# A pre-norm attention and gated MLP block: the down projection of two token tiles from seven block products, the start in another order, and all steps ordered by a table

## The chip, the cores and the metric

The kernel runs on one core of a Trainium2 chip. The metric is the device time in microseconds (us) of one execution. The time before is the median of 3 runs, 788.14 us (785.44 to 790.55). Engines are named as in the profile: PE is TensorE (PEld its weight loads), DVE is VectorE, ACT is ScalarE, POOL is GpSimd, SP issues the DMAs.

## What is computed

The reference, cut to what matters (T = 2048 tokens, D = 512, 32 heads of 16, F = 1376, float32 throughout):

```python
def _A_ref(x, wqkv, wo):              # H = 32; Dh = 16; W = 256
    qkv = (x @ wqkv).reshape(B, S, 3, H, Dh).transpose(2, 0, 3, 1, 4)
    q, k, v = qkv[0], qkv[1], qkv[2]
    scores = jnp.einsum("bhqd,bhkd->bhqk", q, k) * (Dh ** -0.5)
    mask = (idx[:, None] - idx[None, :] >= 0) & (idx[:, None] - idx[None, :] < W)
    p = _softmax(jnp.where(mask[None, None], scores, -1e9), axis=-1)
    o = jnp.einsum("bhqk,bhkd->bhqd", p, v)
    return o.transpose(0, 2, 1, 3).reshape(B, S, D) @ wo

def _B_ref(x, w_gate, w_up, w_down):
    return (_sigmoid(x @ w_gate) * (x @ w_up)) @ w_down

h = x + _A_ref(_layernorm(x), A_wqkv, A_wo)
h2 = h + _B_ref(_layernorm(h), B_w_gate, B_w_up, B_w_down)
```

## The kernel before, in words

**Numbers.** Each float32 matrix product is made of three float16 matmuls: both sides are scaled by a power of two, rounded to a high half, and the remainder is the low half; the products high·high, high·low and low·high are summed in PSUM (`mm3`). So each operand needs a rounding (a cast) and a subtraction, and each weight an absolute maximum first (`bound`, `scale`).

**Stages.** Tokens are in 16 tiles of 128. The start loads x and the weights of q, k, v and o, takes the maxima, normalises and transposes the first tiles on PE. `do_ln`, `do_qk`, `do_v` go over blocks of 256 tokens; `do_s` (scores for the row maxima), `do_st` (scores again, exponentials), `do_pv`, `do_o` and `do_wo` make attention, and `do_wo` leaves x + attention in X, which holds all 16 tiles on the chip. From the middle of this stage on, the weights of gate, up and down are read (`do_amax`), and gate and up are split into halves. The last pool (`open_p2`) opens when attention's buffers are free: the rest is gate, up and down, for pairs of token tiles.

**Gate and up.** `do_ln2` normalises the two tiles of a pair; `do_pair(p, c)` goes over three parts c of F (512, 512 and 352 columns) and gets gate and up of both tiles, a 2 x 2 block product, from seven products of combined blocks instead of eight (the Strassen and Winograd way): seven products of six matmuls each, whose PSUM banks are copied or added into tiles of SQ by ACT and DVE (`copied`, `added`). `gated` applies the sigmoid on ACT, multiplies on DVE or POOL, splits the result into halves in a tile `hr`, and transposes it by DMA into a place `hT`: one transpose for a token tile and part, 48 in all.

**Down.** `do_down(t)` goes over the 11 blocks of F (ten of 128 rows and one of 96) for one token tile: three matmuls of 512 columns each in one PSUM bank (ring `mm`, two banks), then one DVE instruction (L1099) that adds X and writes to RH, and the DMA out. `do_split(n)` loads one such block of w_down and splits it into halves (ACT and DVE, `halves`).

**The order.** The kernel is written as generators; each `yield` states the engines that could do the next step with a cost, what it needs, and the rings of buffers that it takes. `Planner.run` goes through them and takes, at each time of its own clock, the step with the lowest priority number that can start; priorities come from constants `C` and a table of shifts `SHIFT`. The engines' queues are then fixed in that order and run in order, with semaphores between them. Where several engines could do a step, `alt` allows it for the names in `C["alts"]`. Rings: 3 chunks for weights on their way, 3 tiles `hr`, 3 places for normalised pairs (X2).

**The start.** POOL sets constants in the order in which the text has them: the mask, ones in VT, zeros in `mh`, the identity, then zeros for the staging tiles `sq` and for SQ (`zeros`, `clear`, L411 and L417). `normal` computes mean and variance on DVE, and the power −1/2 on POOL (L478); `prep` takes the maxima of a weight (L293 on ACT, L295 on DVE) and splits it (L452, L454).

Of the kernel before, what the change touches and what calls it, by code (L numbers as in the profile page):

```python
# [26 lines left out]
F32 = mybir.dt.float32  # L27
# [24 lines left out]
AHEAD = 2  # L52

PE_, DVE_, ACT_, POOL_, DMA_ = ENGINES = "PE", "DVE", "ACT", "POOL", "DMA"

C = dict(zero=-46.373, s=7.211, pv=-31.68, o=-67.24, wo=[13.21, 53.452], v=[23.818, 127.681], qk=[-13.459, 6.441], ln=[-31.38, -5.584], m=-39.786, am=243.064, amd=116.487, sp=[132.972, 8.062], l2=[-53.459, -314.47], ngu=4, gu=[255.313, 151.063], sp2=[-37.338, 31.729], l2b=-29.57, eps=0.065, prep=[-249.121, -79.126, -27.448, -187.12], alts=['amax', 'cp', 'hhi', 'hi', 'less2', 'lo', 'oadd', 'pt', 'qk', 'raw', 'v', 'whi', 'wsc'], look=-0.248, blog=291.066, bias={'ACT': -74.105, 'DVE': -28.406, 'POOL': -183.807}, pet=8, npv=2, down=167.802, lw=[-144.266, -82.209, -44.544, 78.782], lx=[134.236, 99.816], fill=[197.218, 182.462], clear=69.714, write=-203.887, slack=132.421, stack=-165.218, off={'ln': [-160.407, -74.442, -3.855, -33.644, 18.117, 88.024, 134.307, 85.825], 'qk': [-37.42, -19.282, 102.973, 30.571, 156.591, 137.001, 38.026, 42.788], 'v': [159.08, 126.771, 137.631, -91.406, 127.637, 151.976, 86.279, 51.768], 's': [-65.666, 11.728, -23.007, 22.514, -27.425, -30.856, 15.823, -16.406], 'wo': [59.674, -28.634, 34.768, 157.532, 71.738, 193.098, 45.03, -20.162], 'o': [-100.642, 202.197, -157.044, -26.171, 77.762, -0.239, 84.539, 28.44], 'pv': [-118.465, -136.9, 28.841, -162.287, 81.069, -58.225, 116.111, -106.813], 'm': [120.536, -271.105, -196.395, -173.5, -275.023, 110.942, -102.738, -139.801]}, ld=-120.453, sq=[-52.631, -19.855], slg=-2.394, la=[26.407, 18.616])


SHIFT = [
# [28 lines left out]
]  # L88

LAG = {"PE": 0.2, "DVE": 0.2, "ACT": 0.19, "POOL": 0.1, "DMA": 0.0}  # L90
OWN = {"PE": 0.0, "DVE": 0.06, "ACT": 0.05, "POOL": 0.0, "DMA": 0.0}
TICK = 10.24 / 3
SWITCH = 0.095


class Port(float):
    pass


class Planner:  # L100

# [1148 lines left out]
```

## Time and profile before

| what | us |
|---|---|
| median of 3 runs | 788.14 (785.44 to 790.55) |
| the profiled execution's own time | 787.88 |
| its span in the trace | 786.1 |
| PE, DVE, ACT, POOL busy | 743.5, 557.9, 460.7, 320.6 |
| first matmul of the transposes, first q/k matmul | 11.93, 18.02 |
| first row maximum | 53.35 |
| last pool opens | 467.17 |
| last matmuls begin, last evacuation begins | 780.24, 782.38 |

The profile shows one execution on the chip. Busy times are unions of the intervals of an engine's instructions; "x" is a count; a row of slices shows tenths of the busy share in 40 equal parts of the span. A row of the timeline has the start, the length, the engine, the line, the operation with its tiles, and in brackets the idle time before it and what ended it; instructions of one kind that follow each other stand in one row with their count. A row of the groups has busy time and mean length in ns, then the engine's idle time just before them and the releasers.

### The profile page before, as it was taken

How to read it: one execution, taken by the hardware profiler on the slowest of the kernel's cores; microseconds unless marked ns; L12 is line 12 of the kernel's file. 1: busy time of each engine (PE TensorE's matmuls, PEld its weight loads, DVE VectorE, ACT ScalarE, POOL GpSimd, SP SyncE). 2: the span in 40 equal slices, each digit the busy share in tenths (PEclk: the TensorE clock that was granted, in tenths of full speed). 3: DMA queues.
4: the chain of work that ended last, by engine and by line, in shares of the span. 5: the costliest groups of instructions: out<-in, count | busy, mean ns of one | idle time of the engine just before them, and what ended most of it. 6: DMA issues, size and time to landing. Idle time of an engine off the chain costs nothing.

```text
span 786.1 us, 17989 instructions
## 1 busy us (share of the span) xinstructions
PE 743.5 (95%) x6606; PEld 460.9 (59%) x6606; DVE 557.9 (71%) x1682; ACT 460.7 (59%) x801; POOL 320.6 (41%) x390
## 2 busy tenths in 40 slices
PE   2899989999999999999999997899999999999998
PEld 1577758678777676777655553454454544544453
DVE  5879999959999899999799448885346434613431
ACT  5851768768878878798877647572335223502330
POOL 9731345444645645565569643504304400400000
PEclk9999999999999999999999999999999999999999
DMA  9387393483946999858985429885426521521321
GB/s 327 115 245 213 99 165 68 123 188 93 200 105 180 189 232 234 177 141 189 255 203 103 70 41 281 163 189 96 100 54 92 111 60 28 95 67 40 61 58 42
DMA packets 179383, 107.99 MB, mean 137 GB/s; under 512 B 144288, under 2 KB 153504, under 8 KB 179296
## 3 DMA queue, kind: packets, MB, share of 16 engines
q1 hardware_dynamic: 179296, 106.86, 58.8%
q8 instruction: 51, 0.84, 0.5%
q14 instruction: 36, 0.29, 0.1%
HBM read 42.07 MB, written 17.83 MB: 76 GB/s over the span
## 4 chain that ended last, share of the span: by engine, by line
PE 64%; DVE 12%; issue 8%; ACT 7%; DMA 5%; POOL 3%; DVEq 0%; POOLq 0%; ACTq 0%; SPq 0%
PE mmp L328 24%; PE sp L998 13%; PE pvp L745 7%; PE sp L654 6%; PE stp L998 5%; DVE junk L639 3%; PE pvp L998 2%; PE stp L719 2%; PE stp L709 2%; DMA oT<-whl 2%; DMA x<-hl 2%; PE stp L708 1%; ACT pa L684 1%; DVE mq L639 1%; PE stp L710 1%
## 5 line engine op out<-in xcount | busy, mean ns | idle before, releaser
L639 DVE CUSTOM_DVE_ANT_0 junk<-sp,mask 128x320 bf16<-128x320 f32 (+4 forms) x512 | 207.4, 464 | 13.7 <-PE sp L654 13.3
L684 ACT ACTIVATE pa<-stp,kappa 128x512 f32<-128x512 f32 (+1 forms) x256 | 155.0, 645 | 22.0 <-PE stp L710 18.8
L998 PEld LDWEIGHTS <-x 128*128 128x128 f16 x1008 | 98.2, 98 | 105.1 <-issue 5.4
L998 PE MATMUL sp<-W,x 128*128 128x512 f16 (+1 forms) x612 | 133.2, 361 | 2.1 <-DVE SQ L1021 2.1
L654 PE MATMUL sp<-SK,SQ 96*128 96x256 f16 (+2 forms) x960 | 127.2, 232 | 5.8 <-DVE mq L639 2.7
L328 PE MATMUL mmp<-xT,W 128*128 128x256 f16 x768 | 111.6, 277 | 5.6 <-DVE W L454 2.2
L654 PEld LDWEIGHTS <-SQ 96*128 96x128 f16 x960 | 80.9, 97 | 34.8 <-issue 16.1
L684 ACT ACTIVATE pb<-stp,kappa 128x512 f32<-128x512 f32 x128 | 83.0, 685 | 13.5 <-PE stp L719 12.2
L692 POOL TENSOR_SCALAR_AFFINE_SELECT pa<-pa 128x1024 f32<-128x1024 f32 x56 | 61.4, 1096 | 70.9 <-ACT pa L684 70.7
L328 PEld LDWEIGHTS <-W 128*128 128x128 f16 x768 | 70.8, 99 | 18.3 <-DVE W L454 3.4
L478 POOL TENSOR_TENSOR rs<-rs,nhalf 128x1 f32<-128x1 f32 x32 | 21.7, 685 | 145.5 <-DVE rs L475 142.8
L281 ACT ACTIVATE SQ<-sp 128x512 f32<-128x512 f32 (+1 forms) x45 | 24.4, 544 | 80.1 <-PE sp L998 79.7
L745 PE MATMUL pvp<-pa,VT 128*17 128x128 f32 (+1 forms) x1408 | 62.7, 308 | 0.0
L998 PE MATMUL stp<-W,x 128*128 128x512 f16 (+1 forms) x264 | 57.4, 355 | 3.8 <-DMA W<-wr 2.6
L709 PE MATMUL stp<-SQ,SK 100*128 100x256 f16 x224 | 59.2, 271 | 0.0
L710 PE MATMUL stp<-SQ,SK 100*128 100x128 f16 x256 | 55.4, 218 | 0.1
L1099 DVE SCALAR_TENSOR_TENSOR RH<-mmp,cd,X 128x512 f32<-128x512 f32 x16 | 11.9, 750 | 60.1 <-PE mmp L328 60.1
L745 PEld LDWEIGHTS pvp<-pa,VT 128*17 128x17 f32 x1408 | 37.8, 98 | 23.9 <-issue 2.8
L328 PE MATMUL mmp<-WO,oT 128*128 128x512 f16 x192 | 49.9, 381 | 0.9 <-DMA oT<-whl 0.8
L708 PE MATMUL stp<-SQ,SK 100*128 100x128 f16 x224 | 49.3, 220 | 1.2 <-ACT pb L684 0.5
L328 PE MATMUL mmp<-W,xT 128*128 128x512 f16 x192 | 48.9, 378 | 0.2 <-DVE sk L575 0.2
L719 PE MATMUL stp<-SQ,SK 100*128 100x256 f16 x256 | 46.8, 274 | 1.4 <-ACT pa L684 0.8
(179 smaller groups left out, 1284.2 us busy)
## 6 DMA issues: line engine op xcount, KB each, us to landing
SQ<-sq SPq DMA_DIRECT2D x96, 128.0 KB
wr<-chunk SPq DMA_DIRECT2D x28, 256.0 KB
W<-wr SPq DMA_DIRECT2D x14, 512.0 KB
SK<-mem SPq DMA_DIRECT2D x16, 384.0 KB
chunk<-in_wd_dram SPq DMA_DIRECT2D x20, 256.0 KB
X<-in_x_dram SPq DMA_DIRECT2D x16, 256.0 KB
mem<-sk SPq DMA_DIRECT2D x8, 512.0 KB
out_dram<-RH SPq DMA_DIRECT2D x16, 256.0 KB
```

The lines of the kernel that those rows point to most:

```text
L281: S.activation(out, x, AF.Copy, scale=scale)
L328: PE.matmul(ps, a_of(a, k), b_of(b, k), start=(k == 0 and i == 0), stop=(k == n - 1 and i == 2))
L639: V.tensor_tensor_reduce(out=junk[:, c0:], in0=ps[:, c0:], in1=mask[:, c0:], scale=1.0, scalar=-3.0e38, op0=ALU.add, op1=ALU.max, accum_ou ...
L654: PE.matmul(ps[:, col:col + k1 - k0], q, SK[0:96, (2 * a + hf) % 5, 4 * (p % 2) + j, k0:k1], start=True, stop=True)
L684: S.activation(dst, a, AF.Exp, scale=kappa)
L692: G.affine_select(out=f, in_=f, pattern=[[0, 8], [-1, 128]], compare_op=ALU.is_gt, fill=0.0, base=0, channel_multiplier=1)
L708: PE.matmul(a[:, 0:128], ks(k0, g, j), qs(b, g, j, 0, 128), start=True, stop=True)
L709: PE.matmul(a[:, 128:384], ks(k0 + 1, g, j), qs(b, g, j, 0, 256), start=True, stop=True)
L710: PE.matmul(a[:, 384:512], ks(k0 + 3, g, j), qs(b, g, j, 128, 256), start=True, stop=True)
L719: PE.matmul(a[:, u, :], ks(k0 + 2, g, j + u), qs(b, g, j + u, 0, 256), start=True, stop=True)
L745: PE.matmul(ps[32 * j:32 * j + 17, u, q0:q1], VT[:, kt % 6, 8 * j + g, :], w[:, j, c:c + q1 - q0], start=first, stop=last, skip_group_chec ...
L998: PE.matmul(ps, X2[p % 3][part][:, (a * COUNT[part] + at) * 2 + k, :], W[c][:, b, j, k, :], start=first and k == 0 and i == 0, stop=k == 1 ...
```

## The change

**Down.** `do_down(p)` now works for a pair of token tiles. Ten of the 11 blocks of F are taken as five pairs `PAIRS`, and D as two halves of 256 (`HALF`): for each block pair the two token tiles by two halves of D are a 2 x 2 block product from seven products of three matmuls of 256 columns; the last block of 96 rows is done as before in four pieces of three matmuls. Two PSUM banks of the ring `mm` take the seven sums in turn (`step`), and DVE adds them to X in place in six pieces a pair (`taken` L1279, `high` L1291: four of 256 columns and two of 512), which is then sent out.

```diff
-    def do_down(t):
-        ps = None
-        for f in range(NF):
-            e, *place = yield {PE_: 0.645}, [("h", t, c) for c in range(3)] + [("W", "d", f)], [] if ps else ["mm"]
...
-            mm3(ps, lambda a, f: hT[t, f // 4][:r, a, f % 4, :], lambda a, f: W["d"][:r, a, f, :], f, NF)
...
-        y = RH[:, place % 2].bitcast(F32)
-        V.scalar_tensor_tensor(y, ps, cd, X[:, t, :], op0=ALU.mult, op1=ALU.add)
+    def do_down(p, prio):
+        bank, places = {}, []
+        kinds = [(2, 2, 1)[c] for c in range(3)]
+        def taken(key, which, t, lo, hi, needs, last):
+            e, = yield {DVE_: (hi - lo) / 960 + 0.13}, needs
+            x = home(t)[:, lo:hi]
+            V.scalar_tensor_tensor(x, bank[which][:, :hi - lo], cd, x, op0=ALU.mult, op1=ALU.add)
...
+        def step(which, lo, j, r, half, fresh, needs, extra=()):
...
+            for c in range(3):
+                need = [("h", p, c, r)] + [("W", "d", 2 * c + i) for i in range(kinds[c])] + (needs if c == 0 else [])
...
+                ps = bank[which][:, lo:lo + HALF]
+                for i in range(kinds[c]):
+                    for n, (a, b) in enumerate(((0, 0), (0, 1), (1, 0))):
+                        PE.matmul(ps, hT[p, c, r][:, a, half * kinds[c] + i, :], W["d"][2 * c + i][:, b, j, :], start=fresh and c == 0 and i == 0 and n == 0,
+                                  stop=c == 2 and n == 2, skip_group_check=not fresh)
...
+        e = yield from step("A", 0, 0, 0, 0, True, [("wo", NT - 1 - i) for i in range(2)])
+        plan.add(prio, taken("r1", "A", t1, 0, HALF, [e], None))
+        e = yield from step("B", HALF, 3, 2, 0, True, [])
+        plan.add(prio, high("r5", "B", t2, e))
+        e = yield from step("A", 0, 6, 2, 1, False, [("r1", p)])
+        plan.add(prio, taken("r6", "A", t1, HALF, D, [e], None))
+        yield from step("B", 0, 1, 0, 1, False, [("r5", p)], ((0, 0, 0, False),))
+        e = yield from step("A", 0, 4, 1, 0, False, [("r6", p)])
+        plan.add(prio, taken("r7", "A", t2, HALF, D, [e], None))
+        e = yield from step("B", HALF, 2, 3, 0, False, [], ((0, HALF, HALF, False),))
+        plan.add(prio, taken("r3", "B", t1, 0, D, [e, ("r6", p)], 1))
+        e = yield from step("A", 0, 5, 1, 1, False, [("r7", p)], ((1, 0, 0, False), (1, HALF, HALF, False)))
...
+        plan.add(prio, taken("r4", "A", t2, 0, D, [e, ("r7", p)], 0))
```

**What it multiplies.** `hidden(p, c)` makes, from the gated tiles of the pair, four sums of blocks (`sum_`, L1215) and four rows (`row`): each is cast to its high half, the low half is subtracted, and one DMA transposes it, so there are 96 transposes instead of 48. `do_split(m)` loads two blocks of w_down, makes four differences (`less`) and splits seven blocks of 256 columns into halves, where the two blocks had four of that size.

```diff
+    def hidden(p, c, prio, h1, h2, u1, u2):
...
+        for step, piece in enumerate((row(0, h1[0], n, PADDED[c], A[:1], [], []),
+                                      sum_("S1", s1, a21, a22, ALU.add, A),
+                                      sum_("S2", s2, s1, a11, ALU.subtract, [("S1", q), A[0]]),
+                                      sum_("S3", a21, a11, a21, ALU.subtract, [("S1", q), A[0]]),
+                                      sum_("S4", s4, a12, s2, ALU.subtract, [("S2", q), A[0]]),
+                                      row(2, u1[0][:, :2 * w], 2 * w, 2 * w, [("S2", q)], [("S4", q)], [u1]),
+                                      row(1, h2[0], n, PADDED[c], [("S3", q)], [], [h2]),
+                                      row(3, s4, w, w, [("S4", q)], [("lo", q, 0), ("S3", q)], [h1, u2]))):
...
+    HALF = D // 2
+    PAIRS = ((0, 2), (1, 3), (4, 6), (5, 7), (8, 9))
+    def do_split(m, prio):
...
+        for step, piece in enumerate((part(0, 1, a, [("dload", m, 0)]), part(1, 2, x[1], [("dload", m, 1)]),
+                                      less("D1", a, c, a, [("dpart", m, 0)]), less("D3", c, d, c, [("D1", m), ("dload", m, 1)]),
+                                      less("D2", d, d, a, [("D3", m), ("dpart", m, 1)]), less("D4", b, b, d, [("D2", m)]),
+                                      part(3, 2, x[0], [("D2", m)], 0), part(5, 2, x[1], [("D4", m)], 1))):
```

**Room.** X2 has two places instead of three (`slot = p % 2`), the chunk ring four instead of three. Tiles 10 to 15 of X are written to DRAM after `do_wo`, their place holds transposed hidden rows, and they come back to the places of tiles 0 to 5 once those are out:

```diff
+        if t >= AWAY:
...
+            nc.sync.dma_start(XS[(t - AWAY) * P:(t - AWAY + 1) * P, :], X[:, t, :])
...
+    def bring_back(t):
+        e, = yield {DMA_: 0.475}, [("out", t - AWAY + i) for i in range(2)] + [("spill", t + i) for i in range(2)], [], 1.46
+        nc.sync.dma_start(X[:, t - AWAY:t - AWAY + 2, :], XS[(t - AWAY) * P:(t - AWAY + 2) * P, :].rearrange("(t p) d -> p t d", p=P))
```

**The start.** The identity is made first; one of the two staging tiles is cleared on DVE, the other on POOL; the mask and the zeros of SQ come later; the first loads alternate (x, two of wq, x, two of wq, and so on); all four maxima of wq are taken on ACT.

```diff
+    for i in range(2):
+        (G if i else V).memset(stage[i][0].rearrange("p h j i u t -> p (h j i u t)").bitcast(F32), 0.0)
...
-            t, = yield alt("amax", DVE_, DVE=0.602, ACT=0.67), [(nm, k)]
+            t, = yield {ACT_: 0.77} if nm == "q" else alt("amax", DVE_, DVE=0.602, ACT=0.77), [(nm, k)]
```

On POOL, from the first instruction of the kernel's body to the first powers (`rs` is the variance, `mh` and `sq` staging tiles). Before:

```order
L355 MEMSET mask 128x320
L357 MEMSET VT 128x192
...
L417 MEMSET SQ_73 32x2048
L411 MEMSET sq_105 128x2048
L411 MEMSET sq_103 128x2048
L478 TENSOR_TENSOR rs<-rs,nhalf 128x1 x2
```

and after:

```order
masks.py:197 MEMSET ident 128x128
L439 MEMSET sq_104 128x2048
masks.py:199 ISA
masks.py:199 AFFINE_SELECT ident<-ident 128x128
L446 MEMSET VT 128x192
L455 MEMSET mh_113 128x128
L455 MEMSET mh_114 128x128
L558 TENSOR_TENSOR rs<-rs,nhalf 128x1 x4
```

The mask, one staging memset and the one of SQ have moved from ahead of the power to behind it or to DVE. On ACT, the first instructions (RT takes the high half of a normalised tile, `am` the maxima). Before:

```order
L281 ACTIVATE RT<-chunk 128x512 x2
L293 ACTIVATE W_87,am<-wq 128x512 x4
L281 ACTIVATE xT<-mmp 128x8x128
L293 ACTIVATE W_87,am<-wk 128x512 x2
L452 ACTIVATE W_87<-wq,sq 128x512
```

and after:

```order
L367 ACTIVATE W_87,am<-wq 128x512
L355 ACTIVATE RT<-chunk 128x512
L367 ACTIVATE W_87,am<-wq 128x512 x3
L532 ACTIVATE W_87<-wq,sq 128x512 x3
L367 ACTIVATE W_87,am<-wv 128x512
```

The second normalised tile and the copies of the transposes (xT) have gone from ACT to DVE, and the maxima of wk come later.

**The order of all steps.** The planner's clock, its costs' use and `SHIFT` are gone; `run` goes through a table `ORDER`, whose numbers name the generator to be continued and the engine it gets. All names but one may now use the other engine. The table sets the whole order anew.

```diff
     def run(self):
-        while True:
-            c = [(x[0], x[1], x[2], e, x[3]) for e in ENGINES for x in [self.pick(e)] if x]
...
-            t, _, _, eng, item = min(c, key=lambda x: x[:3])
+        for code in ORDER:
+            self.now = self.roots[code >> 7]
+            item = self.now[code >> 2 & 31]
+            costs, needs, *more = item[1]
+            self.on = next(iter(costs)) if len(costs) == 1 else ENGINES[1 + (code & 3)]
...
     def alt(name, own, **costs):
-        return costs if name in C["alts"] else {own: costs[own]}
+        return costs if name != "xn" or name in C["alts"] else {own: costs[own]}
```

On DVE late in the last stage (SQ holds the products and hidden tiles, `hr` the halves on their way to the transposes, `hl` those of the normalised pair; stp, sp, pvp and mmp are PSUM banks). Before:

```order
L1019 TENSOR_TENSOR SQ_73<-pvp_91,SQ_73 128x512
L1021 SCALAR_TENSOR_TENSOR SQ_73<-stp,SQ_73 128x512
L1021 SCALAR_TENSOR_TENSOR SQ_73<-sp,SQ_73 128x512
L1071 TENSOR_TENSOR SQ_73<-SQ_73 128x512
L288 TENSOR_TENSOR hr_8334<-SQ_73,hr_8334 128x512
L1099 SCALAR_TENSOR_TENSOR RH<-mmp,cd,X 128x512
L1071 TENSOR_TENSOR SQ_73<-SQ_73 128x512
```

and after:

```order
L357 CAST hr_8319<-SQ_73 128x128
L357 CAST hr_8320<-SQ_73 128x256
L357 CAST hr_8321<-SQ_73 128x352
L362 TENSOR_TENSOR hr_8320<-SQ_73,hr_8320 128x256
L1152 TENSOR_TENSOR SQ_73<-pvp_111,SQ_73 128x512
L1154 SCALAR_TENSOR_TENSOR SQ_73<-sp,SQ_73 128x512
L362 TENSOR_TENSOR hl_7008<-chunk,hl_7008 128x256
L362 TENSOR_TENSOR hl_7008<-chunk,hl_7008 128x512
L362 TENSOR_TENSOR hr_8319<-SQ_73,hr_8319 128x128
L1279 SCALAR_TENSOR_TENSOR X<-mmp,cd,X 128x256
L362 TENSOR_TENSOR hr_8321<-SQ_73,hr_8321 128x352
```

The casts have come over from ACT and the subtractions for the normalised pair partly from POOL; the evacuations of the down projection stand among them in smaller pieces. From the opening of the last pool to its end, DVE has 601 instructions instead of 268.

More of the change, by code (lines that the diff above doesn't have):

```diff
@@ L96 @@
+ORDER = [
[221 rows of a table added]
+]
 class Port(float):
@@ L131, in submit @@
-    def submit(self, item):
-        costs, needs = item[4][:2]
-        for k in needs:
-            if not isinstance(k[0], float) and k not in self.done:
-                self.parked.setdefault(k, []).append(item)
-                return
-        times = [k if isinstance(k[0], float) else self.done[k] for k in needs]
-        item[5] = {e: max([0.0] + [t + (OWN if f == e else LAG)[f] for t, f in times]) for e in costs}
-        for e in costs:
-            self.live[e].append(item)
-            self.changed(e)
@@ L250, in run @@
             try:
-                item[4] = item[3].send(value)
+                item[1] = item[0].send(((0.0, self.on), *places))
             except StopIteration:
-                continue
-            self.submit(item)
-        assert not self.parked and not any(self.live.values()), (list(self.parked)[:9], {e: len(v) for e, v in self.live.items()})
+                item[1] = None
+        assert all(item[1] is None for root in self.roots for item in root)
 @with_exitstack
@@ L856, in halves @@
         return t
-    def do_split(n):
-        w, k, r, c = pieces["d"][n]
-        t, place = yield {DMA_: 0.5}, [("scale", "d"), "p2"] + [("parted", c, k) for c in range(AHEAD, 3) for k in range(2)], ["chunk"], D / 700
-        x = chunk(w, k, r, c)
-        hi, lo = (W["d"][:r, h, k, :] for h in range(2))
-        t = yield from halves(hi, lo, x, sc["sd"][:r], D, [t])
-        plan.free("chunk", place, t)
-        plan.mark(("W", "d", k), t)
+    HALF = D // 2
+    PAIRS = ((0, 2), (1, 3), (4, 6), (5, 7), (8, 9))
@@ L940, in do_ln2 @@
     def do_ln2(p, prio):
-        slot = p % 3
-        after = (["p2"] if slot == 2 else []) + ([("x2f", p - 3)] if p > 2 else [])
-        yield {DVE_: 0.0}, ["x2p", ("wo", 2 * p), ("wo", 2 * p + 1)] + after
-        e, (n0, n1), xa = yield from normal(2 * p, [("wo", 2 * p)], "chunk", row, 18, 2)
+        slot = p % 2
+        after = [("x2f", p - 2)] if p > 1 else []
+        own = [("back" if 2 * p >= AWAY else "wo", 2 * p + i) for i in range(2)]
+        yield {DVE_: 0.0}, ["x2p"] + own + after
+        e, (n0, n1), xa = yield from normal(2 * p, [own[0]], "chunk", row, 18, 2)
         xb = row()
```

408 lines of the change are left out of this document (205 added, 203 removed), and 249 rows, old and new, of tables (ORDER, SHIFT).

## The prediction

> **What bounds the kernel now.** I read the page first (busy shares, slices, chain), then the busy time by stretches, then the matmuls one by one. The profiled execution took 787.88 us, the span is 786.1 of it (the rest lies around it), and the median of the runs is 788.14, so the sum below, made against 787.88, may be read against the median as it stands. From the page, the total, the busy times, three rows of slices and the chain's shares:
>
> ```profile
> span 786.1 us, 17989 instructions
> PE 743.5 (95%) x6606; PEld 460.9 (59%) x6606; DVE 557.9 (71%) x1682; ACT 460.7 (59%) x801; POOL 320.6 (41%) x390
> PE   2899989999999999999999997899999999999998
> DVE  5879999959999899999799448885346434613431
> ACT  5851768768878878798877647572335223502330
> PE 64%; DVE 12%; issue 8%; ACT 7%; DMA 5%; POOL 3%; DVEq 0%; POOLq 0%; ACTq 0%; SPq 0%
> ```
>
> PE is busy 95% of the span. It is idle in the first slice and a little around 460 to 500 us. In the last third VectorE and ScalarE have room, in the first two thirds VectorE has almost none. The same by stretches (columns: the length, then PE, weight loads, VectorE, ScalarE, POOL with counts, the granted clock, DMA share, GB/s); 0 to 53.35 is the time up to the first row maximum, 467.2 is where the last pool opens and the gate/up/down stage has the chip for itself:
>
> ```profile
> 0.00:53.35 53.35, 34.35 (x243) 24.19 (x243) 35.94 (x86) 36.23 (x67) 39.73 (x49) 0.97 0.71 229
> 60.00:510.00 450.00, 431.88 (x4958) 299.70 (x4957) 393.05 (x1350) 328.27 (x561) 235.74 (x291) 0.99 0.70 161
> 467.20:786.10 318.90, 307.29 (x1558) 148.47 (x1546) 156.44 (x268) 119.05 (x217) 64.67 (x71) 0.99 0.46 96
> 467.20:520.00 52.80, 46.09 (x259) 21.50 (x248) 43.06 (x76) 33.79 (x61) 21.09 (x22) 0.97 0.96 213
> 600.00:700.00 100.00, 100.00 (x491) 47.87 (x490) 43.73 (x74) 33.81 (x61) 22.61 (x25) 1.00 0.44 80
> ```
>
> From 600 to 700 PE has no gap, at full clock: there the time is the number of matmuls times their spacing. Fewer or shorter matmuls shorten it directly, as long as VectorE, at 44%, stays out of the way.
>
> **The down projection.** The timeline of PE gives the spacing of 512-column matmuls in the last tile, and of 256-column ones with new weights each time in an undisturbed stretch of q/k work; under them stand the q/k matmuls as one group, with their waits:
>
> ```profile
> 770.52 2.75 PE L328 MATMUL mmp<-WD,OS 128*128 128x512 f16 x12
> 773.11 2.11 PE L328 MATMUL mmp<-WD,WO 128*128 128x512 f16 x9
> ...
> 279.78 5.41 PE L328 MATMUL mmp<-xT,W 128*128 128x256 f16 x48
> 285.03 0.58 PE L654 MATMUL sp<-SK,SQ 96*128 96x192 f16 x6
> ...
> L328 PE MATMUL mmp<-xT,W 128*128 128x256 f16 x768 | 111.6, 277 | 5.6 <-DVE W L454 2.2 <-DVE sq L575 1.9 <-ACT xT L281 1.1
> ```
>
> Twelve of 512 start within 773.11 − 770.52 = 2.59 us, 0.216 each; 48 of 256 within 285.03 − 279.78 = 5.25, 0.1094 each. A pair of tiles now takes 2 × 11 blocks × 3 = 66 of 512, or 14.25 us. After: 7 products × 5 block pairs × 3 = 105, and 4 × 3 = 12 for the last block, so 117 of 256, or 12.80 us. That is −1.45 a pair, **−11.6 us** for eight. It breaks even at 14.25/117 = 0.122 a matmul. The other end: over all 768 the busy time a matmul is 111.6/768 = 0.145.
>
> The Trainium skill, "TensorE: Matmul & The Clock Gate", section "Back-to-back issue gap", gives for a stream of weight load and matmul pairs about 81 ns at 128 columns and 131 ns at 512; an estimate from that page, on the line between them, is 98 ns at 256, so a pair would go from 66 × 0.131 = 8.6 to 117 × 0.098 = 11.5 us and the change would lose some 23 us. The rows here, pairs of the same kind, show 216 and 109 ns: the trace does not agree, and decides.
>
> **The head.** Its timeline, the rows on the chain to the first q/k matmul and the first row maximum:
>
> ```profile
> 4.45 0.15 DVE L475 TENSOR_SCALAR rs<-mv 128x1 f32<-128x1 f32 x1
> 5.04 3.63 POOL L411 MEMSET sq<- 128x2048 f32 x2
> 8.75 1.17 POOL L478 TENSOR_TENSOR rs<-rs,nhalf 128x1 f32<-128x1 f32 x2
> 11.78 0.61 ACT L293 ACTIVATE W<-wq 128x512 f16<-128x512 f32 x1
> 18.02 0.59 PE L328 MATMUL mmp<-xT,W 128*128 128x256 f16 x2 [0.53 <-ACT xT L281]
> 53.35 0.23 DVE L639 CUSTOM_DVE_ANT_0 junk<-sp,mask 128x64 bf16<-128x64 f32 x1
> ```
>
> The variance is ready at 4.60, but the power waits on POOL for memsets until 8.75. After the change one of them (1.8 us) and smaller ones stand ahead on POOL, which ends before 4.60: 4.15 us sooner. ScalarE's wq maxima begin at 11.78 only because its queue holds two normalised tiles first; now one of the four goes ahead of the tile and three behind it, and the pass is bounded by the landing of wq. I expect the first q/k matmul at about 12 instead of 18.0. VectorE must keep up: it gets a memset, three copies of transposes and twelve splits, casts and evacuations more and nine instructions fewer, some 5.9 us net at rows like those below, so 41.8 us of work ahead of the row maximum instead of 35.94. With 1 us of start and 5 of waits (17.4 idle now) that is 47.8, 5.5 sooner; the first q/k matmul says 6. I take **−6**, between −2 (8.5 of waits) and −8 (2.5). It is real only if it carries through 60 to 510, where PE is idle 18.1 us of 450 whatever came before. SP's first loads are only interchanged.
>
> **VectorE in the last stage.** Rows of the groups of VectorE there by shape, and, from the whole execution, its copy out of PSUM and its cast:
>
> ```profile
> L1071 DVE TENSOR_TENSOR SQ<-SQ 128x512 f32<-128x512 f32 x32 | 23.9, 752 | 13.2 <-ACT SQ L1067 13.0
> L288 DVE TENSOR_TENSOR hr<-SQ,hr 128x512 f16<-128x512 f32 x32 | 22.8, 722 | 10.7 <-ACT hr L281 10.6
> L1099 DVE SCALAR_TENSOR_TENSOR RH<-mmp,cd,X 128x512 f32<-128x512 f32 x16 | 11.9, 750 | 60.1 <-PE mmp L328 60.1
> L855 DVE SCALAR_TENSOR_TENSOR WD<-chunk,sd,WD 128x512 f16<-128x512 f32 x10 | 7.3, 748 | 0.1
> L1071 DVE TENSOR_TENSOR SQ<-SQ 128x352 f32<-128x352 f32 x16 | 8.6, 535 | 2.9 <-ACT SQ L1067 2.9
> L1021 DVE SCALAR_TENSOR_TENSOR SQ<-stp,SQ 128x352 f32<-128x352 f32 x8 | 4.2, 524 | 8.2 <-ACT SQ L1067 4.7 <-PE stp L998 3.5
> ...
> L285 DVE TENSOR_SCALAR SQ<-sp 128x512 f32<-128x512 f32 x4 | 2.8, 692 | 3.5 <-PE sp L998 3.5
> L283 DVE CAST W<-wv 128x512 f16<-128x512 f32 x1 | 0.4, 417 | 0.0
> ...
> 476.24 1.89 DVE L288 TENSOR_TENSOR hr<-SQ,hr 128x512 f16<-128x512 f32 x3
> ```
>
> By the new order VectorE has 601 instructions there instead of 268: sums of the hidden tiles, 48 hidden rows more in the stage, the high halves and the PSUM copies that ScalarE did, and six evacuations a pair (four of 256, two of 512) for two. Priced by the lines through these rows (two tiles from SBUF 0.752 at 512 and 0.535 at 352, so 0.405 at 256 and 0.23 at 128; out of PSUM 0.692, 0.524, 0.42; casts 0.42 at 512 and in proportion) the 268 come to 156.0, which agrees with the 156.44 measured, and the 601 to **300 us**. When VectorE never waits it is less: the three in a row above took (1.89 − 0.72)/2 = 0.585 a piece instead of 0.722, a ratio of 0.81, so at least 243; a middle value is 272. PE's work becomes 307.29 − 11.6 = 295.7. So the cover of PE is nearly gone, from 156 against 307 to 272 or more against 296. And at the end VectorE can't help: the last pair's down projection (12.8) and the last row out (3.7, below) come after its last sums, so the stage is at least VectorE's work over its busy share, plus 16. In the attention stage that share is 393.05/450 = 0.873. A stage of 315 (my sum) needs work over share of at most 299, such as 272 at 0.91. Inside a pair, bank A's evacuation must end within the one product on bank B that comes next, 15 × 0.109 = 1.64 us; with two pieces of 0.6 ahead of it in VectorE's queue it ends at about that time, with three PE waits, and behind PE's wait stand the next pair's gate and up products. I count **+2** for products that wait for an evacuation (0 to +17: the high end is 272/0.873 + 16 = 328 against 315, with 4 more for a later start).
>
> ScalarE gets less there (119.05 now), so no term. The Trainium skill, "TensorEngine Tiling (Array Packing)", section "PSUM Bottleneck", speaks against the change: it says that PSUM copies can become the bound, and that both ScalarE and VectorE are to do them; the order gives nearly all to VectorE here. The trace before, with both at it and PE without a gap, agrees but doesn't show the other case.
>
> **The opening.** The timeline after 467.2, where PE waits for weights (W) and SP issues two transposes, and the group of the down matmuls that read OS:
>
> ```profile
> 477.88 1.47 PE L998 MATMUL stp<-W,x 128*128 128x512 f16 x6 [2.63 <-DMA W<-wr]
> 480.48 2.64 SPq L1083 DMA_TRANSPOSE hT<-hr  x2
> 480.71 1.47 PE L998 MATMUL pvp<-W,x 128*128 128x512 f16 x6 [1.36 <-DMA W<-wr]
> ...
> L328 PE MATMUL mmp<-WD,OS 128*128 128x512 f16 x192 | 44.7, 379 | 0.0
> ```
>
> W_d's split costs VectorE 15 of 512 and five of 256 in place of ten of 512, 5.8 us more, and six subtractions from POOL 3.5 more. VectorE's 43.06 of 52.80 becomes 52.4: full. PE can run ahead with products meanwhile; I take **+5**, half of the 9.3, bounds 0 and +12. SP gets 48 transposes more, 48 × 1.32 = 63 us of its queue in the stage, and nine transfers for the six tiles that go out and come back. The down matmuls never wait for a transpose now (0.0), and the 12 of a pair take 16 us of SP in some 37. I put it at nothing; if that cover is gone it costs at most what the +17 holds. The normalised pairs get two places instead of three and the hidden ones are given back after two pairs: the products that wait for them stand a pair's work, 37 us, behind on PE's own queue, so nothing.
>
> **The tail.** The last matmuls and the last evacuation:
>
> ```profile
> 780.24 2.11 PE L328 MATMUL mmp<-WD,WO 128*128 128x512 f16 x9
> 782.38 0.75 DVE L1099 SCALAR_TENSOR_TENSOR RH<-mmp,cd,X 128x512 f32<-128x512 f32 x1 [6.37 <-PE mmp L328]
> ```
>
> From 782.4 to 786.1 there is an evacuation and the way out, 3.7 us, kept. Inside the last pair three products wait for an evacuation (0.42 and the two hops) with nothing between: **+1** (0 to +3). The order of the attention stage is new as well: ±0, bounds −6 and +6, a third of its 18.1 idle us.
>
> Sum: −11.6 − 6 + 5 + 2 + 1 = −9.6, so 787.88 − 9.6 = **778 us**.
>
> **The rivals.**
> 1. The extra work of VectorE fits: no loss at the opening, none later. Then −11.6 − 6 + 1 = −16.6: 771. For it: PE without a gap from 600 to 700, and POOL nearly free of work next to VectorE. Against it: 272 of 296.
> 2. VectorE paces the last stage. Its place is the queue of VectorE between 467 and the last pair, where evacuations stand behind sums and splits, and PE's two down banks wait. At 282 us (a third of the way from 272 to 300) and the attention stage's share, 282/0.873 + 16 = 339 instead of 318.9, less 6 of the head: about 802; at 300 it would be 823. It decides over the sum from work over share 299 on, and is slower than before by over 1% from 317 on. For it: the 87% were reached with POOL and ScalarE sharing the work. Against it: VectorE's row has slices of 9 in a row.
> 3. The head's gain is taken back by VectorE, at 90% or more in most slices from 60 to 150: −3.6, so 784.
> 4. Matmuls of 256 columns are held by their weights at 0.145: 117 × 0.145 = 17.0 a pair, +2.7 instead of −1.45, +33 in all: 811. Against it: 48 in a row at 0.109.
>
> **How the numbers follow.** The sum, 778: 0.42 (0.36 faster, 0.06 within 1%). Rival 1, 771: 0.18, faster. Rival 2, 802: 0.27 (0.15 slower, 0.08 within, 0.04 faster, as the share comes out). Rival 3, 784: 0.10, within. Rival 4: 0.03, slower. Faster by over 1% (below 780.3; 1% is about what a measurement of this kernel can tell from none) 0.58, within 0.24, slower (above 796.0) 0.18. The main case by itself spans 770 to 786. The range runs from 764 (rival 1 with the head at −8 and the attention stage at −6, nearly) to 802, the price of rival 2.
>
> **What would show it.** In the changed profile: 256-column down matmuls at 0.109 in a row; the first q/k matmul near 12 and the first row maximum near 48; the last pool opening near 461; VectorE's busy time from there between 243 and 300, with PE's idle time there no more than 20. If PE's idle time stands with VectorE's evacuation or sums as its releaser and exceeds 30, rival 2 holds. Wrong would be the whole sum if PE waits for transposes (SP) or for tiles brought back.

## The result: 851.33 us, slower by 8%

The changed kernel takes 851.33 us (848.17 to 851.68, 4 runs) against 788.01 before, a ratio of 1.0795 with a 95% interval of 1.0751 to 1.0838. Forecast were 778 and faster; the range ended at 802. From the page of the changed kernel come the span, the busy times, the slices of PE, VectorE and the granted clock, and the chain's shares:

```profile
span 849.6 us, 19062 instructions
PE 765.7 (90%) x7014; PEld 509.9 (60%) x7014; DVE 725.9 (85%) x2052; ACT 438.2 (52%) x771; POOL 277.9 (33%) x342
PE   4788889999898899898999999658999999999997
DVE  8988878888888889888987756999999888898983
PEclk9999988999999999999988999979999999999999
PE 51%; DVE 32%; issue 7%; DMA 6%; ACT 1%; POOL 1%; DVEq 1%; SPq 0%; ACTq 0%; POOLq 0%
```

PE has lost its row of nines in the first half, where attention is, and VectorE's share of the chain has gone from 12% to 32%. Four events of the changed kernel's timeline cut the span into the parts that the prediction used (the power on POOL, the first q/k matmul, the first row maximum, the opening of the last pool):

```profile
4.72 0.55 POOL L558 TENSOR_TENSOR rs<-rs,nhalf 128x1 f32<-128x1 f32 x1 [1.00 <-DVE rs L555]
13.85 3.56 PE L402 MATMUL mmp<-xT,W 128*128 128x256 f16 x18 [2.23 <-DVE xT L357]
45.36 0.23 DVE L720 CUSTOM_DVE_ANT_0 junk<-sp,mask 128x64 bf16<-128x64 f32 x1 [0.26 <-PE sp L735]
523.73 0.14 DVE L394 TENSOR_SCALAR cg<-fg 128x1 f32<-128x1 f32 x1
```

| part | before, us | after, us | difference |
|---|---|---|---|
| start to the first row maximum | 53.35 | 45.36 | −8.0 |
| from there to the opening of the last pool ("attention") | 413.8 | 478.4 | +64.6 |
| from the opening to the end ("last stage") | 318.9 | 325.9 | +7.0 |

So the start gained about what was forecast (8.0 to the first row maximum, where 6 were counted). The last stage lost 7.0 where the sum had it 3.6 shorter, and by far the largest loss lies in a part that the prediction had put at nothing. By stretches (length, PE, weight loads, VectorE, ScalarE, POOL, granted clock, DMA share, GB/s), before, in a stretch of attention:

```profile
60.00:455.00 395.00, 383.58 (x4652) 276.84 (x4654) 353.32 (x1284) 296.46 (x504) 210.07 (x263) 1.00 0.69 160
```

and after, with the last stage and a part of it:

```profile
60.00:455.00 395.00, 358.12 (x4060) 252.35 (x4060) 340.61 (x1184) 266.92 (x461) 165.93 (x205) 0.96 0.57 141
...
523.70:849.60 325.90, 301.47 (x1962) 189.71 (x1954) 285.65 (x601) 89.70 (x163) 51.40 (x57) 0.98 0.61 128
...
600.00:700.00 100.00, 100.00 (x639) 62.23 (x637) 91.97 (x209) 24.01 (x44) 6.24 (x9) 1.00 0.58 106
```

In the same 395 us of attention all engines get less done (PE 4060 matmuls instead of 4652), none is full, and PE's clock is granted at 0.96. That looks like two engines that wait for each other, and PE's waits name the partner. Before (us in total, times, longest):

```profile
PE sp L654 <- DVE mq L639: 2.3, 4, 1.0
```

and after:

```profile
PE sp L735 <- DVE mq L720: 27.9, 82, 1.8
```

PE's scores wait for the row maxima, VectorE's `tensor_tensor_reduce` (L639, now L720). Here is VectorE's timeline where several of them follow each other, before:

```profile
199.68 0.49 DVE L639 CUSTOM_DVE_ANT_0 junk<-sp,mask 128x320 bf16<-128x320 f32 x1
200.09 0.08 DVE L639 DVE_READ_ACCUMULATOR2_ANT mq<- 128x1 f32 x1
200.09 0.49 DVE L639 CUSTOM_DVE_ANT_0 junk<-sp,mask 128x320 bf16<-128x320 f32 x1
200.50 0.08 DVE L639 DVE_READ_ACCUMULATOR2_ANT mq<- 128x1 f32 x1
200.50 0.49 DVE L639 CUSTOM_DVE_ANT_0 junk<-sp,mask 128x320 bf16<-128x320 f32 x1
```

and after:

```profile
207.50 0.49 DVE L720 CUSTOM_DVE_ANT_0 junk<-sp,mask 128x320 bf16<-128x320 f32 x1
207.91 0.08 DVE L720 DVE_READ_ACCUMULATOR2_ANT mq<- 128x1 f32 x1
208.14 0.49 DVE L720 CUSTOM_DVE_ANT_0 junk<-sp,mask 128x320 bf16<-128x320 f32 x1
208.56 0.08 DVE L720 DVE_READ_ACCUMULATOR2_ANT mq<- 128x1 f32 x1
208.78 0.49 DVE L720 CUSTOM_DVE_ANT_0 junk<-sp,mask 128x320 bf16<-128x320 f32 x1
```

Each is as long as before, 0.49 us. But before, the next began with the accumulator's read of the one ahead, 0.41 us after its start; now it begins 0.64 us after it, with a gap of 0.15 behind the read. The brackets name no engine for that gap, so the wait is presumably for VectorE itself; the experiments decide. The line of the change that fits is in `do_s`:

```diff
-            junk = swork.tile([P, 320], BF16, name="junk", bufs=2)
+            junk = swork.tile([P, 320], BF16, name="junk", bufs=1)
```

`junk` takes the elementwise output of the reduction, which nobody reads. With one place each reduction would have to wait until the one ahead has finished writing there. The group's rows say how much that is, before and then after:

```profile
L639 DVE CUSTOM_DVE_ANT_0 junk<-sp,mask 128x320 bf16<-128x320 f32 (+4 forms) x512 | 207.4, 464 | 13.7 <-PE sp L654 13.3
```

```profile
L720 DVE CUSTOM_DVE_ANT_0 junk<-sp,mask 128x320 bf16<-128x320 f32 (+4 forms) x512 | 239.5, 468 | 56.5 <-PE sp L735 9.3
```

The same 512 instructions of the same mean length cover 32 us more (they no longer overlap) and have 43 us more of idle time ahead of them: 75 us of VectorE, in a stage that grew by 64.6.

### The profile page after: what moved, and what is told of

Its sections match the earlier page's. It is cut to its first block, busy times and chain, and to the rows that moved or that the text cites. A ratio compares the mean times of both kernels' runs of the same rounds, so it can differ in the third digit from the quotient of the medians.

```text
span 849.6 us, 19062 instructions
## 1 busy us (share of the span) xinstructions
PE 765.7 (90%) x7014; PEld 509.9 (60%) x7014; DVE 725.9 (85%) x2052; ACT 438.2 (52%) x771; POOL 277.9 (33%) x342
## 4 chain that ended last, share of the span: by engine, by line
PE 51%; DVE 32%; issue 7%; DMA 6%; ACT 1%; POOL 1%; DVEq 1%; SPq 0%; ACTq 0%; POOLq 0%
DVE junk L720 17%; PE sp L1131 12%; PE mmp L402 9%; PE mmp L1308 8%; PE pvp L826 6%; PE stp L1131 5%; PE sp L735 4%; PE pvp L1131 2%; PE stp L800 2%; PE stp L790 1%; DVE WD L951 1%; DMA x<-hl 1%; DVE sq L656 1%; PE mmp L1314 1%; DVE W L1021 1%
## 5 line engine op out<-in xcount | busy, mean ns | idle before, releaser
L720 DVE CUSTOM_DVE_ANT_0 junk<-sp,mask 128x320 bf16<-128x320 f32 (+4 forms) x512 | 239.5, 468 | 56.5 <-PE sp L735 9.3
L735 PE MATMUL sp<-SK,SQ 96*128 96x256 f16 (+3 forms) x960 | 146.5, 237 | 37.3 <-DVE mq L720 29.1
L735 PEld LDWEIGHTS <-SQ 96*128 96x128 f16 x960 | 86.9, 99 | 86.9 <-issue 63.9
L778 POOL TENSOR_SCALAR_AFFINE_SELECT pb<-pb 128x512 f32<-128x512 f32 x64 | 42.7, 667 | 71.4 <-ACT pb L765 64.2
L778 POOL TENSOR_SCALAR_AFFINE_SELECT pa<-pa 128x512 f32<-128x512 f32 x64 | 43.3, 677 | 65.3 <-ACT pa L765 65.3
L790 PE MATMUL stp<-SQ,SK 100*128 100x256 f16 x224 | 61.3, 278 | 0.0
L402 PE MATMUL mmp<-WO,oT 128*128 128x512 f16 x192 | 54.5, 405 | 5.5 <-DMA oT<-whl 5.3
L791 PE MATMUL stp<-SQ,SK 100*128 100x128 f16 x256 | 57.0, 223 | 0.2
L362 DVE TENSOR_TENSOR hr<-SQ,hr 128x512 f16<-128x512 f32 (+3 forms) x90 | 52.0, 588 | 2.4 <-ACT hr L355 1.6
L800 PE MATMUL stp<-SQ,SK 100*128 100x256 f16 x256 | 50.5, 283 | 2.2 <-ACT pa L765 2.2
L1197 ACT ACTIVATE SQ<-sp,cg 128x512 f32<-128x512 f32 (+1 forms) x22 | 14.0, 638 | 73.2 <-PE sp L1131 73.2
```

The source lines that it names most:

```text
L402: PE.matmul(ps, a_of(a, k), b_of(b, k), start=(k == 0 and i == 0), stop=(k == n - 1 and i == 2))
L720: V.tensor_tensor_reduce(out=junk[:, c0:], in0=ps[:, c0:], in1=mask[:, c0:], scale=1.0, scalar=-3.0e38, op0=ALU.add, op1=ALU.max, accum_ou ...
L735: PE.matmul(ps[:, col:col + k1 - k0], q, SK[0:96, (2 * a + hf) % 5, 4 * (p % 2) + j, k0:k1], start=True, stop=True)
L778: G.affine_select(out=p, in_=p, pattern=[[0, 4], [1, 128]], compare_op=ALU.is_ge, fill=0.0, base=0, channel_multiplier=-1)
L790: PE.matmul(a[:, 128:384], ks(k0 + 1, g, j), qs(b, g, j, 0, 256), start=True, stop=True)
L791: PE.matmul(a[:, 384:512], ks(k0 + 3, g, j), qs(b, g, j, 128, 256), start=True, stop=True)
```

## The experiments

Theory A: the single place of `junk` is the loss. Theory B, its rival: the new order of the attention stage is (VectorE has more of it, PE's scores come at other times). Beside them stood the question where the gains of the down projection and of the start had gone. Ratios are to the kernel before on the same chip, some 789 us; e1, e2 and e3 ran on one chip, e4 to e8 on another.

**Two places (e1).** Only the place count is undone; the type is a byte wide, for room.

```diff
-            junk = swork.tile([P, 320], BF16, name="junk", bufs=1)
+            junk = swork.tile([P, 320], mybir.dt.uint8, name="junk", bufs=2)
```

> The changed kernel with two places instead of one for the row maximum's discarded output (junk, as before the change; its type is made one byte wide so that both fit). Theory A, the single place costs the 64 us of the attention stage, because each row maximum waits for the write of the one ahead of it: row maxima in a row start 0.41 us apart instead of 0.53 to 0.64, the attention stage (first row maximum to opening of the last pool) falls from 478 to 410-425 us, the total to 785-798. Theory B, the new order of that stage costs it (VectorE gets more there, PE's scores wait): spacing may fall, but the stage stays over 460 and the total over 835.

Measured: 787.74 us, a ratio of 0.9986 (0.9968 to 1.0003) to before. Its timeline:

```profile
196.16 0.48 DVE L720 CUSTOM_DVE_ANT_0 junk<-sp,mask 128x320 uint8<-128x320 f32 x1
196.57 0.08 DVE L720 DVE_READ_ACCUMULATOR2_ANT mq<- 128x1 f32 x1
196.57 0.48 DVE L720 CUSTOM_DVE_ANT_0 junk<-sp,mask 128x320 uint8<-128x320 f32 x1
```

0.41 us apart again. The first row maximum is at 46.56, the last pool opens at 461.34: attention takes 414.8 us, against 413.8 before. In the same order of steps the group of the reductions covers 214.2 us with 12.6 of idle time ahead of it, 69 us less than with one place, and attention is 63.6 us shorter. Theory B falls: with two places the new order costs the stage nothing.

**One place in the kernel before (e2).** The same line the other way, bf16, the old order untouched.

```diff
-            junk = swork.tile([P, 320], BF16, name="junk", bufs=2)
+            junk = swork.tile([P, 320], BF16, name="junk", bufs=1)
```

> The kernel before with one place instead of two for the row maximum's discarded output, its order untouched. Theory A: row maxima in a row 0.53 us apart or more, 512 of them at 0.12 more are 61 us of VectorE, which is at 87% there, so total 830-850. Theory B: within 8 us of 788.

Measured: 881.06 us, a ratio of 1.1159 (1.1140 to 1.1177): more than expected. Its timeline and its group of the page:

```profile
210.44 0.49 DVE L639 CUSTOM_DVE_ANT_0 junk<-sp,mask 128x320 bf16<-128x320 f32 x1
210.85 0.08 DVE L639 DVE_READ_ACCUMULATOR2_ANT mq<- 128x1 f32 x1
211.08 0.49 DVE L639 CUSTOM_DVE_ANT_0 junk<-sp,mask 128x320 bf16<-128x320 f32 x1
```

```profile
L639 DVE CUSTOM_DVE_ANT_0 junk<-sp,mask 128x320 bf16<-128x320 f32 (+4 forms) x512 | 240.4, 470 | 76.5 <-PE sp L654 15.2
```

0.64 apart, and 33 + 63 = 96 us more of VectorE than before for the group; the run is 91.5 us longer. The old order has more row maxima in a row: counted in the timelines, some 420 of the 512 are followed at once by another, and some 360 in the changed order, where other work stands between them and hides a part of the wait. The expectation went by 0.12 us each; it is 0.23 where one follows the other.

**One place, a byte wide (e6).** A control for the type alone.

```diff
-            junk = swork.tile([P, 320], BF16, name="junk", bufs=1)
+            junk = swork.tile([P, 320], mybir.dt.uint8, name="junk", bufs=1)
```

> The changed kernel with its single place, only of the type one byte wide that the first run needed. Theory A (the number of places): 848 to 855, as the changed kernel. If the narrower type itself is what helped: 785 to 800.

Measured: 851.05 us, 1.0776 (1.0746 to 1.0805). The type does nothing; theory A is shown from both sides and with its control.

**The last stage.** What is left is that e1 is no faster than before, although its last pool opens 5.8 us sooner: its last stage takes 327.6 us instead of 318.9. Each stage length is read from one execution. The last stage of the changed kernel and of e6 is the same as that of e1, and took 325.9 and 325.3, so a difference of some 2 us between two runs tells nothing here. The first 80 us, before:

```profile
467.20:547.20 80.00, 73.29 (x398) 35.09 (x387) 62.08 (x110) 45.41 (x82) 30.34 (x33) 0.98 0.84 182
```

and in e1, with all of its last stage:

```profile
461.30:541.30 80.00, 62.23 (x352) 33.02 (x345) 75.66 (x128) 41.69 (x78) 41.52 (x42) 0.89 0.76 184
...
461.30:788.90 327.60, 303.26 (x1962) 190.20 (x1954) 285.60 (x601) 89.54 (x163) 51.40 (x57) 0.97 0.61 127
```

PE is idle 17.8 us of the first 80 (6.7 before), and its clock is granted at 0.89; from there to 700 us it is idle under 1 us. Its waits in the last stage, before:

```profile
PE sp L998 <- DVE SQ L1021: 2.1, 1, 2.1
...
PE stp L998 <- ACT SQ L281: 1.2, 1, 1.2
PE mmp L328 <- DMA oT<-whl: 0.6, 1, 0.6
```

and in e1:

```profile
PE sp L1131 <- DVE SQ L1154: 9.8, 2, 7.4
PE mmp L402 <- DMA oT<-whl: 5.2, 3, 3.0
PE sp L1131 <- ACT SQ L355: 1.9, 2, 1.5
```

VectorE, at 75.66 of 80, is the first suspect. Four runs take work from it (e3, then e4 and e5 on top of e3, and e7 on top of e5), and a last one looks at the start.

e3 puts the casts of the hidden rows and the PSUM copies of gate and up on ScalarE (118 instructions, 111 of them after the opening), with two places:

```diff
-            e, = yield alt("cp", ACT_, ACT=n / 1200 + 0.093, DVE=n / 960 + 0.069), [(name, q)]
+            e, = yield {ACT_: n / 1200 + 0.093}, [(name, q)]
...
-            e, nh = yield alt("hhi", ACT_, ACT=cols / 1200 + 0.093, DVE=Port(cols / 1920 + 0.069)), needs, ["hr"]
+            e, nh = yield {ACT_: cols / 1200 + 0.093}, needs, ["hr"]
```

> As the first of these runs, and the casts of the hidden rows and the copies out of PSUM in gate and up all on ScalarE, in the same order of steps. If VectorE's load sets what is lost in the last stage (325.9 us against 301 of PE work), the stage gets 6 to 14 us shorter than in the first run, most of it in the first 80 us; if weights and transposes (DMA) set it, it is the same within 3 us; if ScalarE's queue is worse placed for it, it is longer.

Measured: 784.34 us, 0.9937 (0.9921 to 0.9953). The last stage is 325.2 us, 2.4 less than in e1 but no less than in e6 (325.3): what was expected if VectorE's load were not the cause. Between the medians e3 is 3.4 us faster than e1; the profiles do not show where. VectorE lost 40 us of work there (285.6 to 245.0), but only 2.3 of it in the first 80 us (75.66 to 73.32), where PE waits.

e4 takes GpSimd's differences and sums over to VectorE as well:

```diff
-            t, = yield alt("dless", POOL_, POOL=0.62, DVE=Port(0.37)), needs
+            t, = yield {DVE_: Port(0.37)}, needs
...
-            e, = yield alt("hsum", DVE_, DVE=Port(w / 960 + 0.07), POOL=w * 0.0021 + 0.08), needs
+            e, = yield {DVE_: Port(w / 960 + 0.07)}, needs
```

> As the third run (two places, casts and copies on ScalarE), and the differences of w_down and the sums of the hidden tiles all on VectorE; GpSimd had 31 of 256 columns of them in the first 80 us of the last stage, 1.0 us each, and VectorE's instructions beside them took 0.91 instead of 0.72 us. Theory C, GpSimd's subtractions hold VectorE up: VectorE gets 31 x 0.41 = 13 us more and loses 12 to 18 of inflation, its w_down splits of 512 fall to 0.6-0.75 us, and the total is 0 to 6 us shorter. Theory D, it is VectorE's own amount: the total is 4 to 12 us longer.

Measured: 784.09 us, 0.9939 (0.9919 to 0.9959), the same as e3 within the intervals, last stage 323.4. The split of w_down on VectorE in the first 80 us, in e3:

```profile
L951 DVE SCALAR_TENSOR_TENSOR WD<-chunk,sd,WD 128x512 f16<-128x512 f32 x15 | 13.5, 910 | 0.3 <-ACT WD L949 0.2
```

and in e4:

```profile
L951 DVE SCALAR_TENSOR_TENSOR WD<-chunk,sd,WD 128x512 f16<-128x512 f32 x15 | 10.9, 738 | 0.0
```

That GpSimd holds VectorE up is borne out: VectorE does 36 instructions more in the first 80 us (156 instead of 120) in about the same time (74.56 us instead of 73.32), because others, these splits among them, take less time without GpSimd's beside them. Theory D (4 to 12 us longer) falls, but the total gains nothing either, the lowest end of what theory C allowed. The Trainium skill, "SBUF — State Buffer", section "Who interferes with whom", says that a VectorE instruction with two SBUF inputs contends with a GpSimd one that reads SBUF; by that rule the splits must get shorter without GpSimd, and the trace agrees (0.910 to 0.738 us).

e5 leaves the low halves of w_down out (ScalarE writes the rounding a second time), on top of e3:

```diff
-        V.scalar_tensor_tensor(lo, x, w, hi, op0=ALU.mult, op1=ALU.subtract)
+        S.activation(lo, x, AF.Copy, scale=w)
```

> As the third run, but the low halves of w_down are written by ScalarE as a second copy of the rounding, so the low halves' values are left out; VectorE is rid of 21 instructions (17 to 18 us) of the opening. If VectorE sets the opening's loss (17 us of PE's idle time in 80, and a clock of 0.9 there), the last stage falls from 325 to 308-317; if weights, transposes or buffers set it, it falls by under 3.

Measured: 782.21 us, 0.992 (0.9885 to 0.9954). Its last stage takes 320.8, 4.4 less than in e3, between the two expectations: a part of the loss is VectorE's split, not most of it. PE is idle 18.6 us in this stage instead of 24.0, and its waits for VectorE (SQ) have gone from 10.4 to 4.6.

e7 leaves the 20 differences of w_down out too:

```diff
         def less(key, out, x, y, needs):
             t, = yield alt("dless", POOL_, POOL=0.62, DVE=Port(0.37)), needs
-            subtract(out, x, y)
```

> As the run with the low halves of w_down on ScalarE, and the 20 differences of w_down's blocks are left out too, so that its combined blocks hold plain ones; VectorE and GpSimd are rid of all that the seven products add to w_down's split. If the preparation of w_down sets what the opening still loses, the last stage falls from 321 (that run) to 309-316. If it doesn't (transposes, weights on their way, buffers, order), it stays at 318-322.

Measured: 779.57 us, 0.9885 (0.9847 to 0.9923), last stage 317.5, 3.3 less than in e5 and again between the two expectations. But PE is idle no less than in e5 (19.5 us of the stage against 18.6): what is shorter is PE's busy time, 298.0 instead of 302.2 for the same 1962 matmuls, with a granted clock of 1.00 instead of 0.94 in the first 80 us. The profiled execution of e7 has a mean clock of 0.999 and took 777.57 us; its other three have 0.991 to 0.994 and took 778.94 to 781.02. So the 3.3 us may be that execution's clock. All of w_down's preparation together is worth 7.7 us between the profiles of e3 and e7, and 4.8 between their medians. (e5 and e7 also multiply other numbers than e3; whether that bears on the clock was not tried.) The first 80 us of e7:

```profile
458.20:538.20 80.00, 65.12 (x412) 36.75 (x404) 59.50 (x113) 58.57 (x112) 22.43 (x27) 1.00 0.87 199
```

and its longest waits of PE in the last stage:

```profile
PE mmp L402 <- DMA oT<-whl: 5.5, 3, 2.7
PE sp L1130 <- DMA W<-wr: 3.3, 2, 2.3
PE sp L1130 <- ACT SQ L355: 3.0, 5, 1.0
PE sp L1130 <- DVE SQ L1153: 1.2, 1, 1.2
```

With VectorE's part down to 1.2 us PE still stands 14.9 us of the 80, now for the transposes of attention's last tiles (oT), weights on their way and ScalarE. Whether their order on SP's queue or the transfers themselves set these 8 us over the 6.7 of before stays open; neither was tried apart.

**The start (e8).** On top of e3, staging tiles and mask are set on GpSimd ahead of the power, as before the change.

```diff
-        (G if i else V).memset(stage[i][0].rearrange("p h j i u t -> p (h j i u t)").bitcast(F32), 0.0)
+        G.memset(stage[i][0].rearrange("p h j i u t -> p (h j i u t)").bitcast(F32), 0.0)
```

(with the mask's memset and its four selects put ahead of the identity).

> As the third run (two places, casts and copies on ScalarE), but at the start both staging tiles and the mask are set on GpSimd ahead of the power, as before the change; loads and maxima keep their new order. GpSimd's memsets then end 2.9 us later. If they set the first q/k matmul, it starts 2 to 3 us later than in the third run and the last pool opens 1 to 3 us later; if the landing of wq sets it, both move by under 1.

Measured: 790.71 us, 1.0018 (0.9997 to 1.0040), 6 us more than e3. Its power and its opening:

```profile
6.80 0.55 POOL L565 TENSOR_TENSOR rs<-rs,nhalf 128x1 f32<-128x1 f32 x1
...
464.95 0.14 DVE L394 TENSOR_SCALAR cg<-fg 128x1 f32<-128x1 f32 x1
```

The power is 2.1 us later than in e3, the first q/k matmul 1.25 (15.05 against 13.80). Both follow from where VectorE begins on the second tile of x (`BATCH_NORM_STATS2`), as the first q/k matmul comes 7.2 us behind that in both: in e3 at 6.58, when the tile has landed; in e8 at 7.84, when VectorE has normalised the first tile behind the late power. So GpSimd's constants set the start in e8, and the landing of the second tile does in e3. The last pool opens 5.5 us later (464.95 against 459.41), outside both expectations: 1.6 us of that stand at the first row maximum (47.12 against 45.52), the rest came in attention, which takes 417.8 us against 410 to 415 in e1, e3, e4, e5 and e7. That is not explained.

## Why the prediction was wrong, point by point

- **The step that failed** is the sentence "The order of the attention stage is new as well: ±0, bounds −6 and +6". About the order it was right: with two places (e1) attention takes 414.8 us against 413.8. But the term was made for instructions that change places, and a change to the instruction itself was not looked for: one place fewer for `junk` adds no instruction, moves none, and is one number in the diff. What the runs showed in its place is a chain: a reduction that directly follows another starts 0.64 us after it with one place (the changed kernel, e2, e6), and 0.41 with two (the kernel before, e1). It was worth +64.6 us in the profiles, and 63.6 between the medians of the changed kernel and e1.
- It could have been priced, if too low. The rows before show reductions 0.49 us long that start 0.41 apart, so they overlap by 0.08, on an engine that is busy for 353.32 of 395 us. Where one VectorE instruction needs the result of the one ahead, two rows of the start show the distance: 0.03 us behind its end.

```profile
15.73 0.15 DVE L311 TENSOR_SCALAR fq<-fq 128x1 f32<-128x1 f32 x1
15.91 0.15 DVE L312 TENSOR_SCALAR fq<-fq 128x1 int32<-128x1 int32 x1
```

  So, as an estimate, a reduction that waits costs 0.08 + 0.03 = 0.11 us more, and 512 of them 56 us of VectorE: enough to turn the forecast round if most of it carried through, though half of the 0.23 measured where one follows another.
- **The down projection: right.** 256-column matmuls follow each other at 0.109 us, as these rows of the changed kernel show (9 within 589.53 − 588.55 = 0.98):

```profile
588.55 1.15 PE L1308 MATMUL mmp<-WD,X 128*128 128x256 f16 x9
589.53 0.82 PE L1308 MATMUL mmp<-WD,OS 128*128 128x256 f16 x6
```

  PE's busy time in the last stage, 307.29 before, is 298.0 in e7, with a granted clock of 1.00: −9.3 of the −11.6. In the changed kernel and e1 it is 301 to 303, at a clock of 0.97 to 0.98, so only 4 to 6 us of the 11.6 arrived there; that the clock would fall was in no term.
- **The head: right in size, in part by luck.** −6 was forecast; with two places the last pool opens at 461.34 (461 forecast), the first row maximum is at 46.56 (48 forecast). That 461 was hit so closely is luck: e3, e4, e5 and e7 have the same start and open at 455.0 to 459.4. And the reason was not the one given. The first q/k matmul came at 13.85 instead of 12, and it was not bounded by the landing of wq: it comes 7.2 us after VectorE begins on the second tile of x, whose load now stands behind two of wq. "Only interchanged" was not free. That row before and then after:

```profile
4.52 0.68 DVE L471 BATCH_NORM_STATS2 st<-X 128x6 f32<-128x512 f32 x1
```

```profile
6.64 0.69 DVE L551 BATCH_NORM_STATS2 st<-X 128x6 f32<-128x512 f32 x1 [0.78 <-DMA X<-in_x_dram]
```

- **The opening: mis-sized.** +5 (0 to +12) was the term. In e1 the last stage is 327.6 where the sum had 315, so 12 too little was counted (10 in e6). Of the 12, 7.6 are busy time of PE (303.26 against 295.7, at the lower clock) and 4.7 its idle time (24.3 against 19.6). w_down's preparation measured 4.8 to 7.7 us (e5 and e7), with the doubt about the clock in e7; the casts and copies, at most 2.4 (e3), are within the scatter. GpSimd's hold on VectorE, 0.91 us a split instead of 0.74, was not in the sum, but taking it away (e4) gained nothing in the total. Nor was PE's wait for the transposes of attention's last tiles, 5.2 us in e1 and 0.6 before.
- **Later evacuations and the tail: right.** From 600 to 700 PE has 100 of 100 beside VectorE at 92%, and the tail is 849.6 − 845.95 = 3.65 us against 3.7. VectorE's busy time in the last stage came out as 285.65, inside the stated 243 to 300; PE's idle time there, 24.4 us, lies between the two signs that were set (20 and 30).
- **The rivals.** The first (771) fell with the loss at the opening, the fourth (811) with 0.109 us a matmul. The second, VectorE as the pace of the last stage, was the nearest in sign, but in the wrong place: VectorE became the pace in attention, and by a wait, not by its amount of work. Taking 40 us from it in the last stage (e3) gave at most 2.4. The third, that the head's gain is taken back, did not come in: with two places the last pool opened 5.8 us sooner.

The version with two places, and with casts and copies on ScalarE, (e3) is faster than both kernels: 784.34 us, 0.6% under the kernel before (0.5% to 0.8%). The whole change with the one line alone undone (e1) is not to be told from the kernel before: 0.9986 (0.9968 to 1.0003).

## What to carry to other kernels

Read a diff for buffer counts first: an output that nobody reads still has a place, and on an engine that is nearly full, one place instead of two turns back-to-back instructions into a chain. To price it, look in the trace for instructions of that kind that overlap, and for a pair that depends on each other; the difference of their distances, times the count, is a first estimate of the cost if the engine has no room (here half of the true one). When a stage slows down and no engine in it is full, look for the wait between two engines and, on the one waited for, for gaps that no other engine explains.

## What the runs showed of the hardware that was not expected

- A VectorE reduction of 320 columns that must wait for the write of the one ahead starts 0.64 us after it, and 0.41 when it need not: 0.23 us for each that follows another at once, alike in the changed kernel, e2 and e6. The Trainium skill, "VectorE: DVE Perf Modes", section "The DRAIN you can't avoid", says of eight copies in a row that a semaphore between VectorE instructions costs nothing extra. For these reductions, where the wait is for the instruction directly ahead, the trace does not agree, and the measurement decides.
- In some stretches PE's waits came with a lower granted clock: 0.96 in attention with one place, 1.00 before, and 0.89 in the first 80 us of e1's last stage, where PE had gaps of up to 7.4 us. Idle time alone doesn't set it: in the first 80 us of e7's last stage PE was idle 14.9 us, in gaps of up to 2.7, and the clock was 1.00.
- With GpSimd's constants ahead of the power (2.1 us later), e8 took 6 us more than e3; 1.25 us of it are traced to the start, the rest is not explained.
